# Attention and two feed-forward layers in one kernel: two weight parts in conversion at a time, three blocks turned by TensorE, layer 2 one unit later

## The chip, the cores and the metric

One NeuronCore of a Trainium2 chip runs the whole program. The metric is the device time of one execution in microseconds (us). Three timed runs before the change gave 2670.62, 2671.53 and 2671.14 us, median 2671.14 us.

The engines are TensorE (PE; PEld is its weight load), VectorE (DVE), ScalarE (ACT), GpSimd (POOL) and SyncE (SP), which issues all DMAs here. PSUM has eight banks, each 128 partitions by 512 words. "L807" is line 807 of the kernel before.

## What is computed

The reference, cut to what matters, with B = 2, C = 128, kv of 384 x 32 places, 24576 queries in all, and DFF = 2048:

```python
kv_pool = kv.reshape(B, 96, 4, 8, 4, C).mean(axis=(2, 4))   # 768 keys per batch
k = v = kv_pool.reshape(B, -1, C) @ w_sr
a = softmax(q @ k.T / sqrt(C));  x = a @ v                  # attention
h = x @ moe_w_in;   x2 = (h * clip(h + 3, 0, 6) / 6) @ moe_w_out      # layer 1
h = x2 @ moe2_w_in; out = (h * cos(h)) @ moe2_w_out                   # layer 2
```

The arrays q and kv are float32. The two layers' weights, moe_w_in, moe_w_out, moe2_w_in and moe2_w_out (in1, out1, in2, out2 in the kernel), arrive as 64-bit words, so each weight is two 32-bit words in memory.

## The kernel before, in words

**Tiling.** The 24576 queries are 48 blocks of 512 (T), 24 per batch. For each block the attention gives a tile x of 128 channels by 512 queries. Each layer then does 8 units (NP) per block; a unit covers 256 of the 2048 hidden values. A unit has a product into the hidden layer (L807 to L809, six matmuls into a pair of neighbouring banks), the gate, and a product out of it (L815 to L817, six matmuls that add into one bank kept for the eight units of the block). Each operand is a pair of rounded tiles, `hi` and `lo`, so each product is three matmuls per half.

Layer 1's gate is ScalarE's relu L822 and VectorE's L825. Layer 2's gate is ScalarE's L830 (whole turns), VectorE's L833 (the rest), ScalarE's sine L839 and VectorE's L842, which is the last reader of the unit's banks. In both layers ScalarE's L869 then makes `hi` and GpSimd's L845 makes `lo`. There are 7 `hi`, 6 `lo` and 13 `w` buffers; the `w` buffers hold most other things, raw weights among them.

**Attention of a block.** Four groups of 128 queries: scores on TensorE (L642, into a pair of banks), row maximum on VectorE (L648), exponential on ScalarE (L654), the inverse of the sum on VectorE, and the normalisation on GpSimd (L669). The probabilities must then be turned. For blocks 0 and 1 (`b < BY_PE`) TensorE does it: 24 transposes of 128x128 (L725), and three copies out of PSUM (L328 on ScalarE or L330 on VectorE); q is turned by four transposes (L557), L560 and L563. For all other blocks it goes through memory: VectorE parts the 16-bit halves (L697, four per block), SyncE stores four pieces (L704) and loads them with three transposing DMAs (L740); q takes GpSimd's L576, two DMAs, L594, and GpSimd's L597. The products with the values are L756; L772 and L779 split the result into the `hi` and `lo` of x.

**Weights.** Each of the four matrices is converted in four parts, 16 parts in all, by `plan_weight`. A part is loaded (SP) and goes through: ScalarE's L358; VectorE's L363, L370, L377; ScalarE's L395 (the `hi` of the weight) beside VectorE's L383 and L390; then VectorE's add L399 and subtraction L402, which gives the `lo`. A part keeps one PSUM bank ("one") and one of TURNS places ("turn") from L358 to L402. With TURNS = 1, one part is in conversion at a time. Two units of a layer need one part of its `in` matrix and one of its `out` matrix.

**Order of the work.** `Plan.run` lays down each engine's order when the program is built. Each operation has a priority (a due time); the planner walks through time with an estimated cost for each, and on each free engine starts the ready operation with the lowest priority whose buffers and banks are free. On the chip the engines run those orders with semaphores. The due times come from the loop at L983: layer 1's unit i and layer 2's unit i - LAG come together, each 2586 apart, and block g's attention is due AHEAD units before its first unit. Weight part k is due at W_FIRST + k * W_STEP, in the order in1, out1, in2, out2. A unit's output is due 28000 behind the unit.

**Gates between sine and exponential.** Both are ScalarE functions of different tables. `last_sine(g)` is g * 8 - AHEAD - LAG (not under 0). Block g's exponentials wait for the sines of the layer-2 units just below that number (L963), and later layer-2 units wait for block g's exponentials (L967).

Of the kernel before, what the change touches and what calls it, by code (L numbers as in the profile page):

```python
# [10 lines left out]
F32 = mybir.dt.float32  # L11
# [5 lines left out]
ALU = mybir.AluOpType  # L17
# [12 lines left out]
G = 1  # L30


LAG = 15
AHEAD = 3

NW, NHI, NLO, NX = 13, 7, 6, 6
SPARE = 5

NSCR = 3

BY_PE = 2

NBANKS = 8

TURNS = 1
ET_SPARE = 2

W_SPARE = 3
# [6 lines left out]
KV_AHEAD, KV_STEP, KV_PROJECT = 200000, 25000, 10000  # L55
WARM = 3
A_STEP = 2000
W_FIRST, W_STEP = 10000.0, 4000.0
HI_AT, LO_AT, OUT_AT = 8000, 4000, 28000
Q_AT, AT_AT, AV_AT, XS_AT = -1000, 6000, 9000, 9000  # L60
ACT_AT, DVE_AT, SIN_AT, MUL_AT = 4000, 200, -2000, -4000
# [43 lines left out]
class Plan:  # L105
# [17 lines left out]
    def op(self, prio, where, emit, after=(), take=(), drop=(), table=None, spare=None):  # L123
        if spare is None:
            spare = self.spare if "dma" in where else 0
        after = [a for a in after if a]
        o = Op(len(self.ops), prio, where, emit, after, take, drop, table, spare)
        self.ops.append(o)
        return o
# [111 lines left out]
def attention_ffn_ffn_kernel(  # L241
# [11 lines left out]
    nc = tc.nc  # L253
# [33 lines left out]
    def tiles(tag, count, shape, dtype, pool=const):  # L287
        return [pool.tile(shape, dtype, name=f"{tag}{i}") for i in range(count)]
# [9 lines left out]
            "s": tiles("s", 8, [P, 4], F32),  # L298
            "turn": list(range(TURNS)),
            "one": free_banks,  # L300
# [8 lines left out]
    op = plan.op  # L309
# [3 lines left out]
    def one(key):  # L313
        return banks[:, plan[key][0], :]
# [6 lines left out]
    ENG = {"act": nc.scalar, "dve": nc.vector, "pool": nc.gpsimd}  # L321

    def flat(t):
        return t.rearrange("p a b -> p (a b)")
# [7 lines left out]

    WK = 4

    def plan_weight(prio, n, src, part):
        raw, tt = ("raw", n, part), ("wt", n, part)
        ks = slice(part * WK, (part + 1) * WK)
        if n.startswith("in"):
            src = src.rearrange("c (k f) -> c k f", f=2 * P)[:, ks, :]
        else:  # L340
            src = src.rearrange("(k f) d -> f k d", f=P)[:, ks, :]
        hi, lo = (x[:, ks, :].rearrange("p k f -> p (k f)") for x in weights[n])

        def words():
            r = flat(plan[raw]).bitcast(I32).rearrange("p (w t) -> p w t", t=2)
            return r[:, :, 0].bitcast(U32), r[:, :, 1]

        def work():

            return one(tt).bitcast(I32)  # L350

        def load(e):
            nc.sync.dma_start(
                out=flat(plan[raw]).bitcast(I32).rearrange("p (k f) -> p k f", k=WK), in_=src
            )

        def magnitude(e):
            nc.scalar.activation(work().bitcast(F32), words()[1].bitcast(F32), AF.Abs)  # L358

        def clamp(e):  # L360

            t32 = work().bitcast(F32)
            nc.vector.tensor_scalar(  # L363
                out=t32, in0=t32, scalar1=SMALLEST, scalar2=None, op0=ALU.max
            )

        def rebase(e):

            t = work()
            nc.vector.tensor_scalar(  # L370
                out=t, in0=t, scalar1=3, scalar2=0x3FFFFFF8,
                op0=ALU.logical_shift_left, op1=ALU.bitwise_and,
            )

        def sign(e):
            top = words()[1]
            nc.vector.scalar_tensor_tensor(  # L377
                out=top, in0=top, scalar=-(1 << 30), in1=work(),
                op0=ALU.bitwise_and, op1=ALU.bitwise_or,
            )  # L380

        def power(e):
            nc.vector.tensor_scalar(  # L383
                out=work(), in0=words()[1], scalar1=-(1 << 23), scalar2=None, op0=ALU.bitwise_and
            )

        def rest(e):

            t32 = work().bitcast(F32)
            nc.vector.scalar_tensor_tensor(  # L390
                out=t32, in0=words()[0], scalar=2.0**-52, in1=t32, op0=ALU.mult, op1=ALU.mult
            )

        def high(e):
            nc.scalar.copy(hi, words()[1].bitcast(F32))  # L395

        def add(e):
            t32 = work().bitcast(F32)
            nc.vector.tensor_tensor(out=t32, in0=t32, in1=words()[1].bitcast(F32), op=ALU.add)  # L399

        def low(e):
            nc.vector.tensor_tensor(  # L402
                out=lo, in0=work().bitcast(F32), in1=hi.bitcast(F32), op=ALU.subtract
            )

        a = op(prio, {"dma": 1560}, load, take=[(raw, "w")], spare=W_SPARE)
        a = op(prio, {"act": 560}, magnitude, [a], take=[(tt, "one"), (("turn", n, part), "turn")])
        a = op(prio, {"dve": 602}, clamp, [a])
        a = op(prio, {"dve": 602}, rebase, [a])
        c = op(prio, {"dve": 602}, sign, [a])  # L410
        a = op(prio, {"act": 520}, high, [c])
        c = op(prio, {"dve": 602}, power, [c])
        c = op(prio, {"dve": 602}, rest, [c])
        c = op(prio, {"dve": 602}, add, [c, a], drop=[raw])
        a = op(prio, {"dve": 602}, low, [c], drop=[tt, ("turn", n, part)])
        for k in range(part * WK, (part + 1) * WK):
            w_ready[n, k] = a

# [124 lines left out]
    def plan_attention(prio, b):  # L543
# [57 lines left out]

        if b < BY_PE:
            a = op(prio - LOAD_AHEAD, {"dma": 1000}, load, take=[(raw, "w")])
# [13 lines left out]
        for j in range(NJ):  # L617
            a = plan_scores(prio + 1000 * j, b, j, q_op, k_ops)
            if b >= BY_PE:
                a, stored = plan_halves(prio + 1000 * j + 500, b, j, a, first)  # L620
# [69 lines left out]
    def plan_halves(prio, b, j, scaled, first):  # L690
        e_, pl, scr = ("e", b, j), ("pl", b, j), ("scr", b)

        def halves(e):
            def words(key):
                return flat(plan[key]).bitcast(U16)[:, 0 : 2 * KEYS]

            ENG[e].tensor_copy(  # L697
                words(pl).rearrange("p (g h k) -> p g h k", g=GK, h=2),
                words(e_).rearrange("p (g k h) -> p g h k", g=GK, h=2),
            )  # L700

        def store(e):
            js = slice(j * 2 * P, (j + 1) * 2 * P)
            nc.sync.dma_start(  # L704
                out=plan[scr][:, js, :].rearrange("g (p h) k -> p g (h k)", h=2),
                in_=flat(plan[pl]).bitcast(U16)[:, 0 : 2 * KEYS].rearrange(
                    "p (g x) -> p g x", g=GK
                ),
            )

        a = op(
            prio, {"dve": 1650}, halves, [scaled, first],
            take=[(pl, "w")] if j else [(pl, "w"), (scr, "scr")], drop=[e_],
        )
        return a, op(prio + 100, {"dma": 900}, store, [a], drop=[pl])

    def plan_weights_t(prio, b, cp, stored):
# [10 lines left out]

        if b < BY_PE:
            a = op(  # L730
# [224 lines left out]
    def last_sine(g):  # L955

        return max(0, g * G * NP - AHEAD - LAG)

# [22 lines left out]
    work = []  # L981
    t = 0.0
    for i in range(-AHEAD, NU + LAG):  # L983
        g, r = divmod(i + AHEAD, G * NP)
        if r == 0 and g < NB // G:
# [8 lines left out]
        if 0 <= i < NU:  # L994
            work.append((t, 3, lambda pr, i=i: plan_unit(pr, 1, *divmod(i, NP))))
            t += UNIT
        if i >= LAG:
            work.append((t, 4, lambda pr, i=i: plan_unit(pr, 2, *divmod(i - LAG, NP))))
            t += UNIT
# [6 lines left out]
    for i, (n, src) in enumerate(  # L1006
        (("in1", w_in1), ("out1", w_out1), ("in2", w_in2), ("out2", w_out2))
    ):
        for part in range(2 * NP // WK):
            plan_weight(W_FIRST + W_STEP * (4 * i + part), n, src, part)  # L1010
    for at, _, fn in work:
        fn(at)
    with tc.manual_schedule():
# [29 lines left out]
```

## Time and profile before

| | |
|---|---|
| timed runs | 2671.14 us median (2670.62 to 2671.53) |
| profiled execution, its own time | 2667.97 us |
| its span, first to last instruction | 2666.2 us |
| granted TensorE clock, mean over the span | 0.995 |
| PE busy | 2613.4 us, 98% |
| ACT busy | 2299.1 us, 86% |
| POOL busy | 2152.9 us, 81% |
| DVE busy | 2089.0 us, 78% |
| DMA moved | 241.77 MB, mean 91 GB/s |

Busy time is the time in which an engine has an instruction in flight. Matmuls overlap each other, so a mean duration of one is longer than its distance to the next. The granted clock is the share of 2.4 GHz that TensorE was given; 0.50 is 1.2 GHz. In a table of stages, each row is one stretch of the span. In a row of waits, the first name is the instruction that waited and the second the one that released it.

### The profile page before, as it was taken

The page shows a single profiled execution, that of the slowest core. Times are in us where ns is not written, and L with a number is a line of the kernel's source. Part 1 is how long each engine was busy: PE and PEld are TensorE (multiplying, and loading weights), DVE is VectorE, ACT ScalarE, POOL GpSimd, SP SyncE. Part 2 cuts the span into 40 slices and gives each one's busy share as a digit, 9 for nine tenths or more (in the row PEclk, how much of TensorE's full clock was granted, in tenths as well). Part 3 has the DMA queues.
Part 4 walks back from the last instruction along what each step waited for, and adds up shares of the span by engine and source line. Part 5 has one row for each costly group of instructions (what it writes and reads, how often), then busy time and mean ns, then how long its engine had stood idle before and what let it go on. Part 6 is the DMA issues. An engine that isn't in the chain of part 4 may idle for free. (4 is left out here: it accounts for less than half of the span.)

```text
span 2666.2 us, 32082 instructions
## 1 busy us (share of the span) xinstructions
PE 2613.4 (98%) x11120; PEld 2064.6 (77%) x11120; DVE 2089.0 (78%) x2185; ACT 2299.1 (86%) x2613; POOL 2152.9 (81%) x1106
## 2 busy tenths in 40 slices
PE   7979999999999999999999999999999999999998
PEld 6657787778877877777777877787778777877787
DVE  8997787778777888877777777777777777777776
ACT  4888988888888888898889988998899888888887
POOL 1768888888888888788888888888888888888788
PEclk9989999999999999999999999999999999999999
DMA  6333334333433354433333343334332343234220
GB/s 191 101 84 77 87 91 104 75 88 89 105 72 91 87 139 111 111 76 89 97 83 87 78 104 85 91 75 100 91 91 72 103 92 91 72 99 91 71 60 28
DMA packets 516323, 241.77 MB, mean 91 GB/s; under 512 B 392256, under 2 KB 490688, under 8 KB 516160
## 3 DMA queue, kind: packets, MB, share of 16 engines
q1 hardware_dynamic: 516160, 239.72, 36.0%
q8 instruction: 87, 1.43, 0.2%
q14 instruction: 76, 0.62, 0.1%
HBM read 33.62 MB, written 109.31 MB: 54 GB/s over the span
## 5 line engine op out<-in xcount | busy, mean ns | idle before, releaser
L845 POOL TENSOR_TENSOR lo<-w,hi 128x1024 fp32r<-128x1024 f32 x768 | 1835.9, 2409 | 418.1 <-ACT hi L869 233.0
L869 ACT CAST hi<-w 128x1024 fp32r<-128x1024 f32 x768 | 793.2, 1051 | 111.3 <-DVE w L842 75.8
L807 PE MATMUL banks<-x,w_in_hi 128*128 128x512 f32 x1536 | 635.4, 414 | 19.5 <-DVE w L842 7.3
L815 PE MATMUL banks<-hi,w_out_hi 128*128 128x512 f32 x1536 | 629.5, 410 | 2.7 <-DVE w L825 2.3
L809 PE MATMUL banks<-x,w_in_hi 128*128 128x512 f32 x1536 | 603.1, 393 | 1.4 <-DVE x L779 1.4
L817 PE MATMUL banks<-lo,w_out_hi 128*128 128x512 f32 x1536 | 600.8, 391 | 2.2 <-POOL lo L845 2.2
L808 PE MATMUL banks<-x,w_in_lo 128*128 128x512 f32 x1536 | 602.0, 392 | 0.8 <-DVE w_in_lo L402 0.8
L816 PE MATMUL banks<-hi,w_out_lo 128*128 128x512 f32 x1536 | 599.3, 390 | 0.0
L842 DVE TENSOR_TENSOR w<-w,banks 128x1024 f32<-128x1024 f32 x384 | 465.2, 1217 | 143.9 <-ACT w L839 143.4
L825 DVE SCALAR_TENSOR_TENSOR w<-w,banks 128x1024 f32<-128x1024 f32 x384 | 462.6, 1216 | 117.3 <-ACT w L822 116.7
L833 DVE SCALAR_TENSOR_TENSOR w<-banks,w 128x1024 f32<-128x1024 f32 x384 | 466.0, 1219 | 108.4 <-ACT w L830 106.9
L822 ACT ACTIVATE w<-banks,three 128x1024 f32<-128x1024 f32 x384 | 423.6, 1118 | 43.3 <-PE banks L809 38.9
L839 ACT ACTIVATE w<-w 128x1024 f32<-128x1024 f32 x384 | 404.9, 1062 | 57.5 <-DVE w L833 55.3
L830 ACT ACTIVATE w<-banks 128x1024 int32<-128x1024 f32 x384 | 390.5, 1024 | 55.9 <-PE banks L809 53.5
L807 PEld LDWEIGHTS banks<-x,w_in_hi 128*128 128x128 f32 x1536 | 290.0, 189 | 119.4 <-DVE w L825 25.9
L815 PEld LDWEIGHTS banks<-hi,w_out_hi 128*128 128x128 f32 x1536 | 288.8, 188 | 79.0 <-issue 10.5
L697 DVE COPY w<-w 128x1536 uint16<-128x1536 uint16 x184 | 317.7, 1746 | 38.6 <-POOL w L669 38.4
L816 PEld LDWEIGHTS banks<-hi,w_out_lo 128*128 128x128 f32 x1536 | 288.8, 188 | 72.7 <-issue 17.2
L808 PEld LDWEIGHTS banks<-x,w_in_lo 128*128 128x128 f32 x1536 | 290.1, 189 | 70.1 <-issue 14.1
L809 PEld LDWEIGHTS banks<-x,w_in_hi 128*128 128x128 f32 x1536 | 289.8, 189 | 64.8 <-DVE x L779 1.8
L817 PEld LDWEIGHTS banks<-lo,w_out_hi 128*128 128x128 f32 x1536 | 288.4, 188 | 64.8 <-POOL lo L845 3.4
L756 PE MATMUL banks<-w,v_all 128*128 128x512 f32 x576 | 270.7, 593 | 0.0
(66 smaller groups left out, 1925.0 us busy)
## 6 DMA issues: line engine op xcount, KB each, us to landing
scr<-w SPq DMA_DIRECT2D x184, 384.0 KB, 2.5
w<-in_kv_dram SPq DMA_DIRECT2D x48, 256.0 KB, 5.0
w<-in_q_dram SPq DMA_DIRECT2D x48, 256.0 KB, 3.1
out_dram<-w SPq DMA_DIRECT2D x48, 256.0 KB, 2.0
scro<-w SPq DMA_DIRECT2D x47, 256.0 KB, 2.0
scrq<-w SPq DMA_DIRECT2D x46, 256.0 KB, 2.3
w<-in_moe_w_in_dram SPq DMA_DIRECT2D x8, 512.0 KB, 5.4
w<-in_moe_w_out_dram SPq DMA_DIRECT2D x8, 512.0 KB, 4.3
```

Of the source, the lines that this page charges most:

```text
L807: nc.tensor.matmul(t[:, i, :], w_hi[:, k, :], xx[:, 0, :], start=True, stop=False)
L808: nc.tensor.matmul(t[:, i, :], w_lo[:, k, :], xx[:, 0, :], start=False, stop=False)
L809: nc.tensor.matmul(t[:, i, :], w_hi[:, k, :], xx[:, 1, :], start=False, stop=True)
L815: nc.tensor.matmul(t, o_hi[:, k, :], h[:, i, :], start=(k == 0), stop=False)
L816: nc.tensor.matmul(t, o_lo[:, k, :], h[:, i, :], start=False, stop=False)
L817: nc.tensor.matmul(t, o_hi[:, k, :], l[:, i, :], start=False, stop=(k == 2 * NP - 1))
L822: nc.scalar.activation(plan[g], two(ps), AF.Relu, bias=three, scale=1.0)
L825: nc.vector.scalar_tensor_tensor(out=plan[g], in0=plan[g], scalar=6.0, in1=two(ps), op0=ALU.min, op1=ALU.mult)
L833: nc.vector.scalar_tensor_tensor(out=plan[g], in0=two(ps), scalar=0.25, in1=plan[g].bitcast(I32), op0=ALU.add, op1=ALU.subtract,)
L842: nc.vector.tensor_tensor(out=plan[g], in0=plan[g], in1=two(ps), op=ALU.mult)
L845: nc.gpsimd.tensor_tensor(out=plan[lo], in0=plan[g], in1=plan[hi].bitcast(F32), op=ALU.subtract)
L869: prio + HI_AT, {"act": 947}, lambda e: nc.scalar.copy(plan[hi], plan[g]), [a],
```

## The change

Five constants change, and `plan_weight` gets an argument. Parts 0 to 7 (k < POOL_PARTS: all of in1 and out1) do the last two steps, add and low, on GpSimd; their L390 writes into the low words of the raw buffer in SBUF, so the PSUM bank and the turn are given back after it, and the raw buffer only after the last step. Two parts may be in conversion at once. Block 2 is turned by TensorE as blocks 0 and 1 are. Layer 2 follows 16 units behind, and attention is due 4 units ahead. Weight parts are due 6000 apart.

```diff
-LAG = 15
-AHEAD = 3
+LAG = 16
+AHEAD = 4
-BY_PE = 2
+BY_PE = 3
-TURNS = 1
+TURNS = 2
+POOL_PARTS = 8
-W_FIRST, W_STEP = 10000.0, 4000.0
+W_FIRST, W_STEP = 10000.0, 6000.0
...
-    def plan_weight(prio, n, src, part):
+    def plan_weight(prio, n, src, part, by_pool):
...
             nc.vector.scalar_tensor_tensor(
-                out=t32, in0=words()[0], scalar=2.0**-52, in1=t32, op0=ALU.mult, op1=ALU.mult
+                out=words()[0].bitcast(F32) if by_pool else t32, in0=words()[0],
+                scalar=2.0**-52, in1=t32, op0=ALU.mult, op1=ALU.mult,
             )
...
         def add(e):
-            t32 = work().bitcast(F32)
-            nc.vector.tensor_tensor(out=t32, in0=t32, in1=words()[1].bitcast(F32), op=ALU.add)
+            t32 = (words()[0] if by_pool else work()).bitcast(F32)
+            ENG[e].tensor_tensor(out=t32, in0=t32, in1=words()[1].bitcast(F32), op=ALU.add)
 
         def low(e):
-            nc.vector.tensor_tensor(
-                out=lo, in0=work().bitcast(F32), in1=hi.bitcast(F32), op=ALU.subtract
-            )
+            t32 = (words()[0] if by_pool else work()).bitcast(F32)
+            ENG[e].tensor_tensor(out=lo, in0=t32, in1=hi.bitcast(F32), op=ALU.subtract)
...
-        c = op(prio, {"dve": 602}, rest, [c])
-        c = op(prio, {"dve": 602}, add, [c, a], drop=[raw])
-        a = op(prio, {"dve": 602}, low, [c], drop=[tt, ("turn", n, part)])
+        if by_pool:
+            c = op(prio, {"dve": 602}, rest, [c], drop=[tt, ("turn", n, part)])
+            c = op(prio, {"pool": 1250}, add, [c])
+            a = op(prio, {"pool": 1250}, low, [c, a], drop=[raw])
+        else:
+            c = op(prio, {"dve": 602}, rest, [c])
+            c = op(prio, {"dve": 602}, add, [c, a], drop=[raw])
+            a = op(prio, {"dve": 602}, low, [c], drop=[tt, ("turn", n, part)])
...
-            plan_weight(W_FIRST + W_STEP * (4 * i + part), n, src, part)
+            k = 4 * i + part
+            plan_weight(W_FIRST + W_STEP * k, n, src, part, k < POOL_PARTS)
```

## Rows read from the trace of the kernel before

**Rows 1.** Stages: stretch, its length, busy us (instructions) by engine; clock, DMA share, GB/s.
```profile
0.00:30.00 30.00, 16.29 (x61) 13.91 (x62) 21.82 (x12) 3.15 (x8) 1.78 (x8) 1.00 0.96 299
30.00:100.00 70.00, 62.71 (x274) 46.30 (x273) 63.75 (x100) 50.37 (x72) 29.68 (x21) 0.95 0.39 96
100.00:140.00 40.00, 39.60 (x171) 31.62 (x170) 37.67 (x48) 35.13 (x41) 33.48 (x16) 1.00 0.38 112
140.00:200.00 60.00, 44.76 (x162) 33.16 (x161) 56.60 (x72) 47.65 (x58) 40.16 (x22) 0.89 0.34 81
200.00:300.00 100.00, 99.38 (x428) 78.78 (x427) 77.01 (x85) 85.77 (x97) 79.37 (x42) 1.00 0.34 84
300.00:2600.00 2300.00, 2291.38 (x9775) 1812.82 (x9774) 1790.19 (x1835) 2024.25 (x2284) 1915.51 (x977) 1.00 0.36 90
2600.00:2666.20 66.20, 59.29 (x261) 47.99 (x259) 41.91 (x37) 52.74 (x57) 52.97 (x24) 0.97 0.09 28
```

The engines stand in the order PE, PEld, DVE, ACT, POOL.

**Rows 2.** The four stretches at half clock before 200 us, PE alone: first, last, sum.
```profile
78.70:85.40 6.70, 5.77 (x14) 0.50 0.97 174
...
187.90:191.20 3.30, 2.88 (x7) 0.50 1.19 220
sum 20.00, PE 16.72; mean PE 4.18
```

**Rows 3.** Waits of PE from 30 to 205 us: us in total, times, longest.
```profile
PE banks L807 <- DVE w L842: 6.9, 3, 2.9
PE banks L807 <- ACT w L654: 3.1, 1, 3.1
PE banks L642 <- DVE w L842: 2.5, 2, 2.1
...
PE banks L642 <- ACT w L654: 1.9, 1, 1.9
...
PE banks L808 <- DVE w_in_lo L402: 0.8, 1, 0.8
```

**Rows 4.** Groups of DVE by shape, 30 to 215 us: busy us, mean ns | idle before.
```profile
L697 DVE COPY w<-w 128x1536 uint16<-128x1536 uint16 x8 | 14.0, 1745 | 1.0 <-POOL w L669 1.0
L399 DVE TENSOR_TENSOR banks<-banks,w 128x512 f32<-128x512 f32 x16 | 11.1, 694 | 0.2
...
L402 DVE TENSOR_TENSOR w_out_lo<-banks,w_out_hi 128x512 fp32r<-128x512 f32 x8 | 5.5, 688 | 0.5
L402 DVE TENSOR_TENSOR w_in_lo<-banks,w_in_hi 128x512 fp32r<-128x512 f32 x8 | 5.5, 685 | 0.2
...
L563 DVE TENSOR_TENSOR x<-banks,x 128x512 fp32r<-128x512 f32 x2 | 1.3, 686 | 0.6 <-ACT x L560 0.6
```

**Rows 5.** Groups of POOL by shape, the same stretch and columns.
```profile
L845 POOL TENSOR_TENSOR lo<-w,hi 128x1024 fp32r<-128x1024 f32 x36 | 85.8, 2401 | 44.7 <-PE banks L817 31.4 <-ACT hi L869 4.0 <-DVE x L779 3.5
...
L597 POOL TENSOR_TENSOR x<-w,x 128x512 fp32r<-128x512 f32 x4 | 5.2, 1295 | 4.4 <-ACT x L594 4.4
L576 POOL COPY w<-w 128x1024 uint16<-128x1024 uint16 x3 | 3.1, 1035 | 0.0
```

**Rows 6.** PE's transposes in order of time: start us, length us, instruction.
```profile
54.53 1.04 PE L725 MATMUL banks<-ident,w 128*128 128x128 f32 x8
55.40 1.88 PE L756 MATMUL banks<-w,v_all 128*128 128x512 f32 x4
```

**Rows 7.** Groups of ACT by shape, 30 to 215 us, columns as in rows 4.
```profile
L328 ACT COPY w<-banks 128x1024 f32<-128x1024 f32 x5 | 5.1, 1024 | 2.6 <-DVE w L697 1.3 <-issue 1.2
```

**Rows 8.** Last conversion step L402: ns min/median/max, first and last start us.
```profile
L402 DVE TENSOR_TENSOR w_in_lo<-banks,w_in_hi x8: 679/682/692, 46.9 to 158.0; 128x512 fp32r<-128x512 f32 x8
L402 DVE TENSOR_TENSOR w_out_lo<-banks,w_out_hi x8: 681/692/692, 92.4 to 213.0; 128x512 fp32r<-128x512 f32 x8
```

**Rows 9.** In order of time, DVE, PE, ACT, PE: start us, length us, instruction.
```profile
146.00 0.69 DVE L402 TENSOR_TENSOR w_in_lo<-banks,w_in_hi 128x512 fp32r<-128x512 f32 x1
...
154.92 0.62 PE L642 MATMUL banks<-k_hi,x 128*128 128x384 f32 x2 [2.10 <-DVE w L842]
...
158.14 1.28 ACT L654 ACT_TABLE_LOAD   x1 [0.46 <-DVE s L648]
...
193.91 1.88 PE L756 MATMUL banks<-w,v_all 128*128 128x512 f32 x4
```

## The prediction, made before the change was run

> **What bounds the kernel now.** The table of stages comes first, because the page's shares are means over stages with different limits. From 300 to 2600 us TensorE is busy 2291.4 of 2300 us; nothing in the change makes it do less there, and only 8.6 us could come back. From 30 to 200 us it is busy 62.7 + 39.6 + 44.8 = 147.1 of 170 us, so 22.9 us are idle [rows 1]. The clock adds to that: after each of four idle spells the granted clock is 0.50 (1.2 instead of 2.4 GHz) for a while, and TensorE works 16.7 us inside these stretches [rows 2]. That work would take half as long at full clock, so 8.4 us more are lost. The opening thus costs 22.9 + 8.4 = 31.3 us, and this is what the change can win. The first 30 us (13.7 us idle) wait for kv, which is not touched.
>
> Next comes who releases TensorE between 30 and 205 us. The largest rows wait for a PSUM bank: matmuls of L807 and L642 wait for the last reader of one, VectorE's L842 (6.9 + 2.5 us) or ScalarE's exponentials L654 (3.1 + 1.9 us). The direct wait for a converted weight, L808 behind L402, is only 0.8 us [rows 3]. VectorE is busy 63.8 + 37.7 + 56.6 = 158.0 of the 170 us, 93%, while GpSimd is at 103.3 [rows 1]. So VectorE's queue is what is full, and conversion is a large part of it: 7 instructions for each of 16 parts, about 0.69 us each [rows 4]. The parts come one behind the other from 46.9 to 213.0 us [rows 8].
>
> Last, the order in time shows where the worst stretch comes from. The third part of w_in2 gets its last step at 146.0, the scores of block 3 start at 154.9, ScalarE changes its table for their exponentials at 158.1, and the first product with the values of block 3 starts at 193.9 [rows 9]. The plan lets block 3's exponentials go only behind the sines of layer-2 units 0 to 5 (8*3 - 3 - 15 = 6 units), and units 4 and 5 need that third part. Until 194 us layer 1 has nothing new from block 3.
>
> **The change part by part.**
> Last steps of 8 parts on GpSimd: VectorE loses 8 x (0.694 + 0.687) = 11.0 us [rows 4]. GpSimd gets 16 instructions of 128x512 with two inputs. The nearest row is L597, same shape and two SBUF inputs, 1.30 us; half an L845 would be 1.20 [rows 5]. The new adds read and write every second word, which no GpSimd row of this shape shows; bounds 1.2 and 2.6 us (twice L597), and I take 1.30, the row nearest in form. Sum 20.8 us, in a stage where GpSimd has 66.7 us free. On the chain of one part that is 2 x (1.30 - 0.69) = 1.2 us more, plus a wait for the L845 in front, up to 2.4 us for each step [rows 5]. The raw buffer goes back later by as much. The multiply L390 writes to SBUF instead of PSUM; both kinds of row are at 0.69, so nothing (bounds -0.1 and +0.1 each).
>
> Two parts at a time: VectorE and ScalarE do the same work, but when one part waits for ScalarE's copy, the other has a step ready. A second PSUM bank is taken, of eight. I cost the bank at nothing, since singles are packed two to a pair: with the running sums of both layers and one part, three singles already break two pairs, and a fourth fills the gap. That cover is gone when a fifth is live (the attention product); bounds 0 and +9 us, worked out under the rivals.
>
> Three blocks turned by TensorE: block 2 loses four L697, 4 x 1.745 = 7.0 us of VectorE [rows 4], L576 and L597 on GpSimd (2.3 us) [rows 5], and on SP's queue four stores, three transposing loads and the two for q; the weight loads queued behind them go sooner, if buffers allow. It gains L563 on VectorE, 0.7 us [rows 4], three copies L328 of 1.02 us on ScalarE [rows 7], and on TensorE 24 + 4 transposes. Eight take 55.40 - 54.53 = 0.87 us in a row [rows 6], so 28 take 3.05 us. TensorE is the limit of the whole, so I charge them in full: +3.1 (bounds 0, where they fall into idle time, and +5, with waits for banks between).
>
> VectorE in all: -11.0 - 7.0 + 0.7 = -17.3 us of 158.0.
>
> AHEAD 4 and LAG 16: block 3's exponentials now wait for 8*3 - 4 - 16 = 4 sines, hence for two parts of w_in2 instead of three. One part takes about (213.0 - 46.9)/15 = 11 us on average [rows 8], so block 3 can start some 11 us sooner. At the end one more unit of layer 2 runs without layer 1. The last stretch has 66.2 - 59.3 = 6.9 us idle with 15 such units [rows 1], so I estimate +0.5 (bounds 0 and +2). In the long middle the order shifts by a unit; 8.6 us idle bounds the gain, and I take 0 with 4 us either way.
>
> W_STEP 6000: parts come due later, the last at 100000 instead of 70000. VectorE then serves gates and row maxima before conversions of layer 2. This costs nothing as long as w_out2 is there for layer 2's first outputs; its first part (the thirteenth) is due at 10000 + 12*6000 = 82000, and unit 0's output at 3*2000 + 17*2586 + 28000 = 77962. A late part would hold `lo` buffers, of which there are six. Bounds -5 and +5; I take 0.
>
> What comes back: at most 31.3 us. VectorE's 17.3 us would be the gain if its queue alone set the pace; ScalarE (133.2 of 170 us busy [rows 1], plus 3) and GpSimd (103.3 plus 18.5) have room for that. I take 16, a little under the VectorE sum and half the loss, because table changes, the DMA round trip of block 3 and its bank waits remain. What is late next is that round trip.
>
> Sum against the profiled execution (span 2666.2, its own time 2668.0): -16 + 3.1 + 0.5 = -12.4, hence 2655.6. The three timed runs have a median of 2671.1, 3.2 above the profiled one; taken from that, 2658.7. I predict **2659 us**; its own range is 2651 to 2666.
>
> A rule that speaks against the change: the Trainium skill, "GPSIMD Engine Reference", section "Engine selection", puts elementwise work with two inputs on VectorE and calls GpSimd about twice as slow. The rows agree on the ratio (1.30 against 0.69). By the rule the moved steps lose wherever a part is awaited; this is the second rival.
>
> **Rivals.**
> 1. All of it opens: conversion is early enough and block 3 comes early, so idle time and half clock nearly vanish: 27 of 31.3 us. 2671.1 - 27 + 3.6 = 2648. For it: with later dues part of the conversions moves behind 200 us, where VectorE is only 77% busy [rows 1]. Against: without that it would be 140.7 of 143 us busy.
> 2. The moved steps stand on the path: each of 8 parts is awaited 1.2 us longer, +9.8, so 2659 + 10 = 2669, no change. For it: block 0's units need w_in1 at once, and GpSimd's queue puts an L845 of 2.4 us in front. Against: TensorE waits for converted weights under 1 us now [rows 3].
> 3. The second bank turns it slower: between 140 and 200 us a fifth single leaves one pair. A layer-2 unit holds its pair from its first matmul to L842; TensorE then stands still for its readers. The four waits on banks above sum to 14.4 us [rows 3]; if the gain fails and they grow by two thirds, some 9 us, the time is 2671 + 3.6 + 9 = 2684. It decides from the point where layer 2 runs while two parts convert and attention products are live. For it: banks are already the largest releaser. Against: parts 0 to 7 give their bank back before the GpSimd steps. The Trainium skill, "Trainium Kernel Development and Optimization", section "Best Practices", says that repeated gaps can mean that PSUM ran out. The trace agrees so far as the rows of bank waits go.
> 4. The time from block 3's scores to its first product, 193.9 - 154.9 = 39 us of DMA round trip and table changes [rows 9], is what keeps TensorE short, and less conversion only moves the idle time: gain 3, cost 3.6, 2672. Against: the start of those scores hangs on the conversions too.
>
> **How the numbers follow.** Forecast 0.50, rival 1 0.15, rival 2 0.12, rival 4 0.07, rival 3 0.16. What this measurement can tell from no change is 0.2%, 5.3 us: 2665.8 to 2676.5. Faster: the first two, and part of rival 2's spread, less the forecast's tail: 0.66. Same: 0.18. Slower: 0.16. The range takes in rival 1 with 3 us of the middle's shift below, and most of rival 3 above: 2645 to 2682.
>
> **What would show it.** VectorE's busy time falls by about 17 us over the run, GpSimd's rises by about 18, TensorE's busy time changes by the 3 us less what half clock gives back. TensorE's idle time between 30 and 200 us falls from 22.9 to about 10, with fewer stretches at 0.50. Block 3's scores start before 145 us instead of 154.9. Rows of the two steps on GpSimd at 1.3 us; 2.6 would favour rival 2. Waits of L807 and L642 on L842 and L654 above 14.4 us in the opening would favour rival 3. The forecast is wrong if the stage to 300 us ends no earlier, or if the middle loses more than 4 us to the new order, which no row of before can show.

## The result, and the profile after

The changed kernel takes **2644.93 us** (median of four runs, 2642.96 to 2647.72), the kernel before 2671.34 us beside it: ratio 0.9902, 95% interval [0.9885, 0.9919]. That is 26.4 us less, where 12.4 were forecast. The profiled execution of after is the slowest of its four (2647.7), that of before ran 3.4 us under its median; so the two spans, 2666.2 and 2645.9, differ by 20.3 us only, and these are what the traces can explain; the other 6 us are in no trace here. Because that trace of after is 2.8 us over its median, losses of after set beside those of another run are high by about as much.

Stages of the kernel after, in the columns of [rows 1]:

```profile
0.00:30.00 30.00, 14.96 (x52) 11.90 (x52) 22.31 (x12) 2.87 (x7) 0.73 (x7) 1.00 0.97 246
30.00:100.00 70.00, 58.00 (x242) 42.66 (x243) 60.05 (x101) 50.38 (x75) 43.14 (x33) 0.93 0.32 106
100.00:140.00 40.00, 40.00 (x183) 31.59 (x182) 37.67 (x57) 30.02 (x39) 29.65 (x17) 1.00 0.29 80
140.00:200.00 60.00, 56.39 (x227) 43.58 (x226) 47.70 (x52) 51.84 (x60) 47.20 (x23) 0.94 0.23 57
200.00:300.00 100.00, 99.49 (x432) 79.58 (x430) 80.65 (x84) 93.50 (x105) 86.80 (x46) 1.00 0.40 95
300.00:2600.00 2300.00, 2294.59 (x9845) 1831.35 (x9845) 1789.53 (x1851) 2025.24 (x2288) 1925.54 (x981) 1.00 0.36 89
2600.00:2645.90 45.90, 40.25 (x176) 32.05 (x174) 27.02 (x25) 34.15 (x38) 36.17 (x17) 0.98 0.13 41
```

From 140 to 200 us TensorE is busy 56.4 instead of 44.8 us and VectorE 47.7 instead of 56.6, but from 30 to 100 us TensorE is busy less (58.0 instead of 62.7). Now the row of 300 to 2600 us: busy time rose by 3.2 us only, yet 9845 matmuls began in it instead of 9775. Seventy matmuls at some 0.23 us are 16 us of work. Busy time does not show them, because a matmul stays in flight for longer than its turn. Two neighbours of the kernel before, in order of time:

```profile
1500.90 0.39 PE L808 MATMUL banks<-x,w_in_lo 128*128 128x512 f32 x1
1501.13 0.40 PE L809 MATMUL banks<-x,w_in_hi 128*128 128x512 f32 x1
```

The second begins 0.23 us behind the first, which is marked 0.39 us long. A wait of up to 0.16 us between the two would leave no gap in the busy row. So I use another measure. Each matmul is charged its usual distance to the next (0.2267 us for the layers' products, 0.428 for a product with the values, 0.1745 for scores, 0.32 and 0.109 for the few others), and what is left of a stretch is its **loss**: waits, time at half clock, and matmuls that follow each other more slowly than usual. The span is then the charged work plus the losses:

| us | work | loss 0-300 | 300-2550 | 2550-end | span |
|---|---|---|---|---|---|
| before | 2557.7 | 63.5 | 36.6 | 8.4 | 2666.2 |
| after | 2560.7 | 56.2 | 21.7 | 7.3 | 2645.9 |
| difference | +3.0 | -7.3 | **-14.9** | -1.1 | -20.3 |

Three quarters of these 20.3 us come from the middle, where the prediction had counted on no gain. What gave way there shows on the weight loads, which come before each matmul and are short. Groups of weight loads from 300 to 2550 us, kernel before (busy us, mean ns | idle before, and what ended it):

```profile
L807 PEld LDWEIGHTS banks<-x,w_in_hi 128*128 128x128 f32 x1339 | 251.8, 188 | 90.4 <-DVE w L825 22.0 <-DVE w L842 8.2 <-issue 7.2
```

And after, where L807 is L814, L825 is L832 and L842 is L849:

```profile
L814 PEld LDWEIGHTS banks<-x,w_in_hi 128*128 128x128 f32 x1344 | 252.4, 188 | 68.2 <-issue 9.1 <-DVE w L849 5.3 <-DVE w L832 3.6
```

L807 is the first matmul of a unit and must have a free pair of banks. Before, it waits 22.0 us for layer 1's gate L825 and 8.2 for layer 2's L842 to give one back; after, 3.6 and 5.3. That is 21 us less in waits for these two (some of this time runs beside matmuls still in flight, so it is not all loss).

The 7.3 us of the opening are a balance: from 140 to 200 us the loss falls from 23.4 to 7.8 us, from 30 to 100 us it rises from 13.2 to 22.2. TensorE's waits of the kernel after from 30 to 205 us, as in [rows 3]:

```profile
PE banks L732 <- DVE w L392: 3.7, 1, 3.7
PE banks L814 <- DVE w L832: 3.6, 5, 1.3
PE banks L814 <- DVE w L849: 3.4, 1, 3.4
PE banks L732 <- POOL w L676: 1.9, 1, 1.9
...
PE banks L649 <- ACT w L661: 0.8, 2, 0.5
...
PE banks L814 <- ACT w L661: 0.4, 1, 0.4
```

L649 are the scores and L661 the exponential (L642 and L654 before). The waits on L842 and L654 have fallen from 14.4 to 4.6 us (3.4 + 0.8 + 0.4), while L832, layer 1's gate, now takes 3.6. New is L732, the turning of the probabilities, behind L392: that is the conversion step after which a part gives its PSUM bank back. Block 0's first product with the values comes at 63.5 us instead of 50.1. With one part at a time it comes at 51.4 (e5 below), with block 2 not turned by TensorE at 53.7 (e7), so both together hold block 0 up. Two stretches at half clock are left before 200 us. The first lies over these waits (idle 1.9 and 0.7 us just ahead of it, 3.7 inside), the second behind 3.4 us of waiting for L849 (PE alone, as in [rows 2]):

```profile
53.10:63.20 10.10, 6.44 (x30) 0.50 0.10 27
176.00:182.70 6.70, 5.68 (x13) 0.50 0.94 199
sum 16.80, PE 12.12; mean PE 6.06
```

The moved steps, groups of GpSimd from 30 to 215 us as in [rows 5] (L402 is the add, L406 the subtraction):

```profile
L852 POOL TENSOR_TENSOR lo<-w,hi 128x1024 fp32r<-128x1024 f32 x38 | 90.7, 2408 | 19.5 <-ACT hi L876 17.4 <-issue 1.6 <-ACT w L829 0.3
...
L402 POOL TENSOR_TENSOR w<-w 128x512 f32<-128x512 f32 x8 | 8.3, 1042 | 6.9 <-DVE w L392 5.8 <-DVE s L669 1.1
L406 POOL TENSOR_TENSOR w_out_lo<-w,w_out_hi 128x512 fp32r<-128x512 f32 x4 | 5.2, 1308 | 0.1
L406 POOL TENSOR_TENSOR w_in_lo<-w,w_in_hi 128x512 fp32r<-128x512 f32 x4 | 5.2, 1297 | 0.2
```

The last steps, as in [rows 8]: the last part is done 65 us sooner than before, at 148.5 instead of 213.6.

```profile
L406 POOL TENSOR_TENSOR w_in_lo<-w,w_in_hi x4: 1289/1295/1308, 50.6 to 64.9; 128x512 fp32r<-128x512 f32 x4
...
L406 DVE TENSOR_TENSOR w_out_lo<-banks,w_out_hi x4: 677/684/692, 124.2 to 147.8; 128x512 fp32r<-128x512 f32 x4
```

And block 3 in order of time, as in [rows 9]: its scores start later than before, not sooner.

```profile
158.23 0.62 PE L649 MATMUL banks<-k_hi,x 128*128 128x384 f32 x2
...
161.16 1.28 ACT L661 ACT_TABLE_LOAD   x1
...
190.71 1.88 PE L763 MATMUL banks<-w,v_all 128*128 128x512 f32 x4
```

### The profile page after: what moved, and what is told of

Read it like the earlier page. It is cut to its first block, busy times and chain, and to the rows that moved or that the text cites. A ratio compares the mean times of both kernels' runs of the same rounds, so it can differ in the third digit from the quotient of the medians.

```text
span 2645.9 us, 31989 instructions
## 1 busy us (share of the span) xinstructions
PE 2603.7 (98%) x11148; PEld 2072.7 (78%) x11148; DVE 2064.9 (78%) x2176; ACT 2288.0 (86%) x2606; POOL 2169.2 (82%) x1120
## 4 chain that ended last, share of the span: by engine, by line
PE 90%; DVE 5%; ACT 2%; issue 1%; DMA 1%; SPq 0%; POOLq 0%; POOL 0%; DVEq 0%; ACTq 0%
PE banks L814 12%; PE banks L824 12%; PE banks L823 12%; PE banks L816 12%; PE banks L815 12%; PE banks L822 12%; PE banks L763 9%; PE banks L649 7%; DVE w L832 1%; DMA w<-in_kv_dram 1%; DVE sum L456 1%; DVE w L849 1%; DVE w L704 1%; ACT w L829 1%; DVE w L840 1%
## 5 line engine op out<-in xcount | busy, mean ns | idle before, releaser
L814 PE MATMUL banks<-x,w_in_hi 128*128 128x512 f32 x1536 | 623.1, 406 | 10.7 <-DVE w L849 4.9
L849 DVE TENSOR_TENSOR w<-w,banks 128x1024 f32<-128x1024 f32 x384 | 464.3, 1218 | 177.7 <-ACT w L846 177.5
L816 PE MATMUL banks<-x,w_in_hi 128*128 128x512 f32 x1536 | 600.7, 391 | 0.0
L832 DVE SCALAR_TENSOR_TENSOR w<-w,banks 128x1024 f32<-128x1024 f32 x384 | 462.0, 1214 | 58.9 <-ACT w L829 58.8
L814 PEld LDWEIGHTS banks<-x,w_in_hi 128*128 128x128 f32 x1536 | 289.1, 188 | 91.2 <-DVE w L832 11.1
L823 PEld LDWEIGHTS banks<-hi,w_out_lo 128*128 128x128 f32 x1536 | 288.5, 188 | 74.6 <-issue 20.8
L822 PEld LDWEIGHTS banks<-hi,w_out_hi 128*128 128x128 f32 x1536 | 288.5, 188 | 74.4 <-issue 12.4
L704 DVE COPY w<-w 128x1536 uint16<-128x1536 uint16 x180 | 310.8, 1746 | 32.8 <-POOL w L676 32.3
```

The lines of the kernel that those rows point to most:

```text
L814: nc.tensor.matmul(t[:, i, :], w_hi[:, k, :], xx[:, 0, :], start=True, stop=False)
L816: nc.tensor.matmul(t[:, i, :], w_hi[:, k, :], xx[:, 1, :], start=False, stop=True)
L822: nc.tensor.matmul(t, o_hi[:, k, :], h[:, i, :], start=(k == 0), stop=False)
L823: nc.tensor.matmul(t, o_lo[:, k, :], h[:, i, :], start=False, stop=False)
L832: nc.vector.scalar_tensor_tensor(out=plan[g], in0=plan[g], scalar=6.0, in1=two(ps), op0=ALU.min, op1=ALU.mult)
L849: nc.vector.tensor_tensor(out=plan[g], in0=plan[g], in1=two(ps), op=ALU.mult)
```

## The experiments

All results first; medians in us, ratio to the kernel before with its 95% interval, losses as above, and the end of the last conversion. The charged work is 2560.7 us where block 2 is turned by TensorE, 2557.7 elsewhere (e1, e3, e4, e7, e9, e18).

| run | time | ratio | 0-300 | 300-2550 | converted by |
|---|---|---|---|---|---|
| e1 order alone | 2666.22 | 0.9981 [0.9972, 0.9990] | 75.7 | 24.6 | 206.7 |
| e2 old order | 2657.62 | 0.9947 [0.9930, 0.9964] | 55.0 | 32.8 | 164.5 |
| e3 lag alone | 2709.81 | 1.0144 [1.0129, 1.0159] | 67.6 | 73.6 | 208.4 |
| e4 lead alone | 2671.58 | 0.9999 [0.9989, 1.0008] | 69.1 | 36.0 | 211.6 |
| e5 one turn | 2657.89 | 0.9951 [0.9936, 0.9966] | 67.5 | 20.1 | 226.3 |
| e6 none on GpSimd | 2653.32 | 0.9934 [0.9919, 0.9949] | 62.2 | 21.8 | 159.0 |
| e7 two blocks | 2646.05 | 0.9908 [0.9891, 0.9924] | 59.3 | 20.5 | 180.2 |
| e8 step 4000 | 2652.52 | 0.9932 [0.9917, 0.9947] | 61.7 | 21.9 | 150.9 |
| e9 gate 20 | 2690.43 | 1.0078 [1.0063, 1.0093] | 67.1 | 53.8 | 212.2 |
| e10 gate 18 | 2684.37 | 1.0055 [1.0040, 1.0070] | 51.4 | 62.5 | 139.5 |
| e11 15 with 5 | 2665.50 | 0.9982 [0.9972, 0.9991] | 51.6 | 41.9 | 147.8 |
| e12 16 with 3 | 2693.97 | 1.0092 [1.0077, 1.0107] | 48.7 | 70.3 | 156.2 |
| e13 16 with 5 | 2665.16 | 0.9976 [0.9967, 0.9985] | 55.7 | 40.4 | 166.4 |
| e14 17 with 5 | 2665.22 | 0.9977 [0.9968, 0.9986] | 55.1 | 42.0 | 162.7 |
| e15 all on GpSimd | 2640.86 | 0.9886 [0.9871, 0.9900] | 51.2 | 21.7 | 173.9 |
| e16 later dues | 2644.25 | 0.9899 [0.9882, 0.9916] | 51.6 | 22.0 | 156.5 |
| e17 e15 and e16 | 2643.01 | 0.9892 [0.9877, 0.9908] | 53.8 | 20.7 | 180.7 |
| e18 e17, two blocks | 2649.52 | 0.9921 [0.9909, 0.9934] | 60.8 | 22.1 | 178.4 |

**Where the middle's gain comes from: e1 to e4.** Order theory against conversion theory.

e1, on the kernel before:
```diff
-LAG = 15
-AHEAD = 3
+LAG = 16
+AHEAD = 4
```


> The kernel before with LAG 16 and AHEAD 4 and nothing else of the change. Order theory (the two constants remove short waits of TensorE all through the middle, 15 us between 300 and 2600 us): about 2656 us, the work left on TensorE gaining about 15 us on the kernel before between 300 and 2600 us. Conversion theory (the gain is that conversions end at 148 instead of 214 us, and the middle only passes on that head start): about 2671 us, no gain in the middle.

The middle gains 12.0 us (36.6 to 24.6) without any change to the conversion, so the order theory holds there; the other 2.9 of the 14.9 come with the rest of the change (24.6 to 21.7). The total of 2656 was missed: the opening loses 12.2 us more under the new order when conversion is as slow as before. The weight loads of L807 from 300 to 2550 us look like those of after:

```profile
L807 PEld LDWEIGHTS banks<-x,w_in_hi 128*128 128x128 f32 x1346 | 252.7, 188 | 69.7 <-issue 8.8 <-DVE w L842 6.6 <-DVE w L825 4.5
```

e2 is the reverse on the kernel after (LAG 15, AHEAD 3).

> The changed kernel with LAG 15 and AHEAD 3 again. Order theory: only the opening's gain stays, 4 us (up to 12 if the old order suits the opening better), so 2659 to 2667 us. Conversion theory: 2645 to 2650 us.

2657.6, just under what the order theory gave and far from the other; the middle is back at 32.8, and so are most of the waits on layer 1's gate (groups of weight loads of e2, 300 to 2600 us; L832 is L825):

```profile
L814 PEld LDWEIGHTS banks<-x,w_in_hi 128*128 128x128 f32 x1375 | 258.2, 188 | 90.2 <-DVE w L832 21.7 <-DVE w L849 7.4 <-issue 6.7
```

Conversion and turning alone take 8.5 us of loss from the opening (63.5 to 55.0) and add 3.0 of work; under the new order they take 19.5 (75.7 to 56.2).

e3 and e4 set one constant each, on the kernel before (`LAG = 16`; `AHEAD = 4`).

> The kernel before with LAG 16 alone. If the lag (16 is two whole blocks, so both layers change blocks at the same unit) carries the middle's gain: 2655 to 2660 us. If the earlier attention carries it: 2669 to 2674 us. Conversion theory: 2671 us.

> The kernel before with AHEAD 4 alone. If the earlier attention carries the middle's gain: 2655 to 2660 us. If the lag carries it: 2669 to 2674 us. Conversion theory: 2671 us.

Neither carries the gain: the lead alone does nothing, and the lag alone loses 37 us more in the middle. There it is the scores that wait for banks: 45.1 us idle before them in e3 against 12.5 in the kernel before (groups of weight loads, 300 to 2550 us; L642 are the scores). Of e3:

```profile
L807 PEld LDWEIGHTS banks<-x,w_in_hi 128*128 128x128 f32 x1319 | 247.9, 188 | 92.5 <-DVE w L825 15.2 <-DVE w L842 12.9 <-issue 10.5
...
L642 PEld LDWEIGHTS banks<-k_hi,x 128*128 128x128 f32 x656 | 120.3, 191 | 45.1 <-DVE w L825 33.4 <-DVE w L842 2.4
```

Of the kernel before:

```profile
L642 PEld LDWEIGHTS banks<-k_hi,x 128*128 128x128 f32 x672 | 122.4, 188 | 12.5 <-DVE w L825 0.8
```

**What the opening is made of: e5 to e8**, each one part of the change undone in the kernel after.

```diff
-TURNS = 2
+TURNS = 1
```


> The changed kernel with one part in conversion at a time (TURNS 1). If two at a time is what brings the end of conversion from 214 to 148 us, it ends behind 180 us here, block 0's first product with the values comes near 50 us instead of 63.5, and the loss between 140 and 200 us comes back: 2650 to 2658 us. If VectorE's shorter work does it (prediction): conversion ends before 165 us and the time is 2641 to 2648 us. The middle should stay within 4 us of the changed kernel in both cases.

Two at a time is the largest part: 13.0 us. Conversion ends at 226.3, block 0's product comes at 51.4, and from 140 to 200 us VectorE is full again, TensorE at 44.3 (stage of e5, columns of [rows 1]):

```profile
140.00:200.00 60.00, 44.29 (x177) 33.45 (x176) 58.51 (x72) 48.90 (x58) 36.08 (x20) 0.91 0.33 87
```

```diff
-POOL_PARTS = 8
+POOL_PARTS = 0
```


> The changed kernel with all 16 parts ending on VectorE (POOL_PARTS 0). If VectorE's queue sets the pace of the opening, its 11.0 us come back in part: 2650 to 2657 us. If the moved steps stand on the path (1.30 against 0.69 us each, behind an L845), taking them back gains or costs nothing: 2638 to 2646 us.

8.4 us slower than after. Each step is longer on GpSimd, and moving it there still gains, so it is VectorE's queue and not the length of the steps that counts on balance.

```diff
-BY_PE = 3
+BY_PE = 2
```


> The changed kernel with only blocks 0 and 1 turned by TensorE (BY_PE 2). If block 2's early turning is worth VectorE's 7 us: 2648 to 2655 us. If its 28 transposes and its share of the first 60 us cost more than that: 2635 to 2642 us, with block 0's first product with the values before 60 us.

Neither: 1.1 us. The loss of the opening is 3.1 us larger, the work 3.0 smaller. Block 0's product does come before 60 us (53.7), but what is won there is lost again by 200 us: from 30 to 200 us TensorE is busy 154.5 us in e7 and 154.4 in after.

```diff
-W_FIRST, W_STEP = 10000.0, 6000.0
+W_FIRST, W_STEP = 10000.0, 4000.0
```


> The changed kernel with weight parts due 4000 apart (W_STEP 4000). If the later dues spare the gates of the first units: 2648 to 2656 us, conversion ending before 140 us. If they do nothing: 2643 to 2648 us.

The later dues are worth 7.6 us, though conversion ends at almost the same time (150.9). How is not shown: with the earlier dues TensorE falls behind most from 140 to 200 us (52.5 us busy instead of 56.4), and there VectorE is busy less, not more (44.1 instead of 47.7).

**Which part of the order: e9 to e14.** LAG and AHEAD set two things, the due times and the gate. e9 and e10 part them: the constants set the gate and the order in which operations are declared, and the due times come from the same loop with the other pair. e9, on the kernel before (e10 the reverse on the kernel after):

```diff
-LAG = 15
-AHEAD = 3
+LAG = 16
+AHEAD = 4
...
+    DUE_LAG, DUE_AHEAD = 15, 3
...
+    due = {key: t for t, _, key in schedule(DUE_LAG, DUE_AHEAD)}
...
-    for at, _, fn in work:
-        fn(at)
+    for _, _, fn, key in work:
+        fn(due[key])
```


> The kernel before, all due times as with LAG 15 and AHEAD 3, but the gate between sines and exponentials at 8 g - 20, where LAG 16 and AHEAD 4 put it. Gate theory (the place of ScalarE's table change in the block decides whether outputs are left to fill TensorE): the middle gains 10 to 15 us on the kernel before. Due theory (the due times of the two layers and of attention decide): the middle stays within 4 us of the kernel before. The opening moves by some us either way, so the loss between 300 and 2550 us decides: 36.6 before, 21.6 changed.

> The changed kernel, due times of LAG 16 and AHEAD 4, but the gate at 8 g - 18 as before. Gate theory: the middle loses 32 to 40 us as before the change. Due theory: 20 to 25 us.

Both theories fall. The gate (with its order of declaration) alone makes the middle worse (53.8), and so do the due times alone (62.5). In e10 the first matmuls wait 46.3 us for layer 1's gate:

```profile
L814 PEld LDWEIGHTS banks<-x,w_in_hi 128*128 128x128 f32 x1320 | 247.8, 188 | 119.9 <-DVE w L832 46.3 <-issue 12.4 <-DVE w L849 8.1
```

Other pairs, all in the kernel after (e11 `LAG = 15`, `AHEAD = 5`; e12 `LAG = 16`, `AHEAD = 3`; e13 16 and 5; e14 17 and 5):

> The changed kernel with LAG 15 and AHEAD 5: the gate stays at 8 g - 20, the layers are 15 units apart, attention is due one unit sooner. Gate theory: the middle loses 18 to 25 us, the total 2641 to 2650 us. If the lag of two whole blocks is what counts: 30 us or more, 2653 to 2662 us.

> The changed kernel with LAG 16 and AHEAD 3 (gate 8 g - 19), the setting that lost 73.6 us in the middle without the conversion change. If the loss of the middle depends on the two constants alone: some 73 us again, 2690 to 2700 us. If the opening had set it off: under 45 us, below 2670 us.

> The changed kernel with LAG 16 and AHEAD 5. If a lead of at least 4 units with a lag of two whole blocks is what the middle needs: the loss between 300 and 2550 us stays at 18 to 25 us, 2641 to 2650 us in all. If 16 with 4 is a lone fit: over 30 us, above 2653 us.

> The changed kernel with LAG 17 and AHEAD 5, both one more, the difference of 12 as in both kernels. If the difference of lag and lead counts: 18 to 25 us lost in the middle, 2641 to 2651 us. If 16 with 4 is a lone fit: over 30 us, above 2653 us.

e12 repeats e3's loss with another opening (70.3 against 73.6), and all ten kernels with 16 and 4 (after, e1, e5 to e8, e15 to e18) lose 20 to 25; the old pair loses 36.6 and 32.8 (before, e2). So the middle follows, within some 4 us, from the constants and not from the opening. Neither the gate at 8g - 20 (e11) nor the lag of two blocks (e12, e13) nor the difference of 12 (e14) is enough. Of the seven pairs that ran, 16 with 4 is the only one that loses under 30 us in the middle.

**More of the opening: e15 to e18.** On the kernel after: e15 `POOL_PARTS = 16`; e16 `W_FIRST = 20000.0`; e17 both; e18 both with `BY_PE = 2`.

> The changed kernel with the last two steps of all 16 parts on GpSimd. If VectorE's queue still sets the pace of the opening: 11.0 us less for it, 2636 to 2643 us. If GpSimd's queue is what holds the parts of layer 2 back (it is 75 to 79% busy from 100 to 200 us): 2645 to 2655 us.

The best version: 2640.86, 1.1% less than before, 4.1 us under after's median. From 100 to 140 us VectorE drops to 30.3 of 40 us, and from 140 to 200 us GpSimd is nearly full while TensorE stays busy for 57.6 us (stages of e15):

```profile
100.00:140.00 40.00, 38.95 (x175) 30.19 (x175) 30.34 (x43) 31.43 (x39) 38.69 (x25) 1.00 0.17 53
140.00:200.00 60.00, 57.55 (x246) 45.02 (x244) 48.24 (x53) 53.79 (x63) 58.45 (x34) 1.00 0.32 79
```

> The changed kernel with all weight parts due 10000 later (W_FIRST 20000). If the parts take VectorE and two banks from block 0's attention: its first product with the values comes near 52 us instead of 63.5, the work left at 60 us is 7 to 10 us less, and 2636 to 2643 us in all unless conversion then ends too late. If that order comes from elsewhere: no change at 60 us, 2643 to 2649 us.

Half right: block 0's product comes at 56.4 and the loss of the opening is 4.6 us under that of after's trace, but the time, 2644.25, is after's within its runs.

> The changed kernel with POOL_PARTS 16 and W_FIRST 20000. If they gain by different means (GpSimd spares VectorE, the later due spares block 0): 2633 to 2638 us. If both only bring the same idle time back: 2639 to 2644 us. The middle loses 20 to 25 us in both cases.

> The same with BY_PE 2. If block 2's turn on TensorE is worth nothing: within 3 us of e17. If VectorE still sets the pace of the opening: 4 to 8 us slower than e17. The middle loses 20 to 25 us.

They don't add up; e17 is no better than e15. Beside them block 2's turn on TensorE is worth 6.5 us (e18), where alone it was worth 1.1 (e7). The middle stayed at 20.7 and 22.1.

## Why the prediction was wrong

The direction was right and the size was not: 2659 was forecast and 2644.9 measured. Against the sum of the prediction, the opening of the trace brought 8.7 us too little and the middle 14.9 that the sum did not have, so two errors partly cancel. Step by step:

**The step that failed: "nothing in the change makes it do less there, and only 8.6 us could come back", and with it "I take 0 with 4 us either way" for the middle.** It read TensorE's idle time as its loss. The loss was 36.6 us from 300 to 2550 us; most of it lay under the busy marks (8.6 us of those 2250 were idle). The middle gave back 14.9 us, and e1 shows 12.0 of them with LAG and AHEAD alone. The Trainium skill, "Perfetto Trace Analysis", section "Identifying the Most-Contended Engine", says that matmul busy time is a poor measure of how close TensorE is to its limit; the trace agrees, 99.6% busy with 1.6% lost. The row that shows it is the idle time of the weight loads by releaser: 22.0 us behind L825 stood there before the change.

**The opening: "I take 16".** By loss it gave 7.3, and up to 6 more if all that no trace holds lies there. It is a sum of two things. The new order alone costs the opening 12.2 us (e1), which the prediction did not see. On top of that order, conversion and turning took 19.5; on the old order 8.5 (e2). So 16 lies between what the same edits bring in two orders.

**VectorE's 17.3 us less, as the reason.** Partly right. VectorE's queue did bear on the time (e6, e15). But the largest part got no term of its own: a second turn, 13.0 us (e5). With one part at a time, VectorE's shorter list does not end conversion sooner: 226.3 us in e5, with all other edits in. Nor was VectorE full all the while: from 100 to 140 us it was busy 27.2 of 40 us there. The one place for a part stood empty from 66.0 to 81.0 and from 93.9 to 112.9 us, and the load of the seventh part was issued at 99.9 us, in after at 65.7. Why the parts began so late with one turn is not shown.

**"Block 3 can start some 11 us sooner."** Wrong: its scores began at 158.2 instead of 154.9. The stretch from 140 to 200 us recovered with two parts at a time: in the six kernels that convert one part at a time (before, e1, e3, e4, e5, e9) conversion ends behind 206 us and TensorE is busy there for 38.4 to 45.7 of 60 us, in all others conversion ends by 181 us and TensorE is busy for 52.3 to 58.1.

**W_STEP "I take 0".** It is worth 7.6 us (e8), outside the bounds of 5 either way.

**Turns by TensorE, +3.1.** 3.0 of work, as said; with VectorE's relief the edit came out about even in e7 (1.1 us gained). **The moved steps, 20.8 us:** 8 x (1.04 + 1.30) = 18.7. **The end, +0.5:** -1.1.

**The signs.** Busy time of VectorE over the run fell by 24.1 us where 17 were named, GpSimd's rose by 16.3 (18 named), and TensorE's idle time from 30 to 200 us fell from 22.9 to 15.6, not to 10.

**The rivals.** The moved steps on the path: refuted by e6 and e15. The second bank: its wait is there once, 3.7 us behind L392, and block 0 is 13 us late; but the second turn brings 13.0 us more than it costs (e5). The round trip of block 3: 190.7 - 158.2 = 32.5 us instead of 39, and TensorE is short there no longer. "All of it opens" named nearly the right time, 2648, for a reason that did not occur: 56.2 us of loss stayed in the opening, some 32 of them behind the first 30 us, and 14.9 us came from the middle.

**What stays open.** Why 16 with 4 fits and the six other pairs do not. In each of the six the first matmuls of the units wait longer for a pair of banks behind the last readers of the gates (20.7 to 30.2 us for L825 and L842 together, from 300 to 2550 us, against 8.9 in after and 11.1 in e1; in e3 and e12 the scores wait too), but which work is missing to fill these places was not isolated.

## What to carry to other kernels

Ask how much work began, not how long the engine was marked busy: count instructions per stage, or charge each its usual distance, and read the waits on the weight loads. When an order is planned by due times and gates, constants that set several of them must be tried together; one alone can cost more than the pair gains. And where a chain of short steps hops between engines, a second one in flight can be worth more than shortening the first (here 13.0 against 8.4 us, e5 and e6).

## What the runs showed of the hardware

GpSimd's add of two interleaved word planes of one buffer, 128x512 float32 in place, took 1.04 us; the subtraction with a contiguous second input and fp32r output took 1.30, as long as L597 before, whose inputs are both contiguous. Reading every second word did not cost GpSimd anything that these rows show. With GpSimd busy for 58.5 of 60 us (e15, 140 to 200 us), TensorE was busy for 57.6, against 56.4 with 47.2 in after.
